# Attention beside a gelu MLP: a constant by memset, weight magnitudes on ScalarE, seven V projections inside the blocks

## The chip, the cores and the metric

The kernel runs on one core of one Trainium2 chip. The metric is the device time of one execution in microseconds; 0.3% of it is 4.5 us. Names used below: TensorE (PE; its weight loads are PEld), VectorE (DVE), ScalarE (ACT), GpSimd (POOL) and SyncE (SP), whose queue issues all of the kernel's DMAs. PSUM has eight banks of 128x512 fp32; TensorE writes there and VectorE and ScalarE read it out.

## The reference

One sequence of 2048 rows and 512 columns. Both branches read the same normalised x.

```python
def _A_ref(x, wqkv, wo):                      # 32 heads of 16
    qkv = (x @ wqkv).reshape(B, S, 3, H, Dh).transpose(2, 0, 3, 1, 4)
    q, k, v = qkv[0], qkv[1], qkv[2]
    scores = jnp.einsum("bhqd,bhkd->bhqk", q, k) * (Dh ** -0.5)
    p = _softmax(scores, axis=-1)
    o = jnp.einsum("bhqk,bhkd->bhqd", p, v)
    return o.transpose(0, 2, 1, 3).reshape(B, S, D) @ wo

def _B_ref(x, w1, b1, w2, b2):                # 512 -> 1792 -> 512
    h = _gelu(jnp.einsum("bsd,df->bsf", x, w1) + b1)
    return jnp.einsum("bsf,fd->bsd", h, w2) + b2

xn = _layernorm(x)
return x + _A_ref(xn, wqkv, wo) + _B_ref(xn, w1, b1, w2, b2)
```

## The kernel before

**Numbers.** Dense products (projections, MLP, output projection) are made in fp16 with every operand split into a high and a low half; `PAIRS` lists the three partial products kept, so a projection of depth 512 is 12 products of 128 rows by 512 columns. Before a weight is split it is scaled by a power of two; `scales` finds it from the largest magnitude. Scores are one fp16 product over stacks: a *stack* (`kst` for keys, `qst` for queries) holds for two heads, in 64 partitions each, the halves of K or Q in 48 rows, and in rows 62 and 63 a constant (`MROW`, 1024, in the keys) against the negative row maximum in two halves (in the queries). Exponentials and V stay in fp32.

**Units.** Work is cut into 512 units: 8 groups of four heads, 4 query blocks of 512, 16 key tiles of 128. A unit u makes four score halves for row maxima (`s_half`, `reduce_max` at L260 on VectorE, tile `mt`), and, 19 units later (`LEAD`), the four transposed score tiles with their exponentials (`e_half`, L305 on ScalarE) and the product with V (`v_half`). The maxima of a block of 16 units are joined at its end (`s_end`, tile `mneg`), turned on TensorE and sent by two DMAs through DRAM into the query stacks.

**Halves.** V products use one half of the array's rows at a time (64 partitions). On the other half, `dense` places products of a dense group, four column tiles each; how many a half unit takes is the group's *pace*: `FAST` is 4, `SLOW` 3, `MEAN` 3 and 4 in turn. So a unit carries 32, 24 or 28 dense column tiles. Groups come from a filler, in this order: Q and K projections for m = 1 to 3 (`rest`), then per query block 14 groups of the first MLP layer and 4 of the second (`mlp`), then the output projection (`tail`). In the units 16 to 18, before the first exponential, `LFILL` places 36 products of the filler's first groups at full width. What the filler has left when the units end is made after them.

**Prologue.** Ahead of the blocks stand the layernorm (`stats`), the transposes of x into `xt` (L799, evacuated at L800 to L806), the projections of Q and K for m = 0 (`project`), all 16 V tiles (`v_proj`, L531, evacuated at L534) and the first 16 units' score halves (`tile_and_unit`). Its order on each engine is found by a planner from estimated costs; from `manual_schedule` on, the order is the one in which the program is written. SP's queue is in order too, and a DMA that waits for a buffer holds those behind it.

**Weights.** The 16 chunks of w1, w2 and wo (512 KB each, tile `wch`, three buffers) are loaded twice: once to find the largest magnitudes (`measure`, two VectorE passes over 128x512 a chunk, L729, tile `amx`), and once to be split on GpSimd (`prepare`, `split_steps`). `MEASURE` says how many passes stand behind each tile of the prologue; the eight passes that are left stand in the first units of the blocks.

**Constants.** `clear` sets both kinds of stacks to zero on GpSimd (L86) and then writes rows 62 and 63 of the key stacks from a small tile by 32 DMAs (L88), 16 for each of two sets of stacks.

Of the kernel before, what the change touches and what calls it, by code (L numbers as in the profile page):

```python
# [1 line left out]

# [15 lines left out]
P = 128  # L18
S = 2048
D = 512  # L20
H = 32
# [8 lines left out]
VW = DH + 1  # L30
LEAD = 19
FAST, MEAN, SLOW = (4, 4), (3, 4), (3, 3)
MEASURE = (3, 0, 1, 2)
HALF = 1300
POOL_NS = 2500
TAIL = 5
LFILL = (8, 16, 12)
WARM = (14, 3, 2, 2)
FINE = "fine"
ORDERED = {mybir.EngineType.SP, mybir.EngineType.PE, mybir.EngineType.Activation, mybir.EngineType.DVE, mybir.EngineType.Pool}  # L40
GELU_C = 0.7978845608028654
GELU_A = 0.044715
MROW = 1024.0
W = 2 * P


@with_exitstack
def layer_kernel(ctx: ExitStack, tc: tile.TileContext, x, wqkv, wo, w1, b1, w2, b2, out):
# [23 lines left out]

    ident = const.tile([P, P], F32, name="ident")
    make_identity(nc, ident)
    ones_row = const.tile([2, P], F16, name="ones_row")
    nc.vector.memset(ones_row, MROW)


    kst, qst = ([[[const.tile([P, QB], F16, name=f"{x}st{i}_{p}_{b}") for b in range(NQB)] for p in range(2)]
# [2 lines left out]
    def clear(i):  # L82
        for b in range(NQB):
            for p in range(2):
                for st in (kst[i][p][b], qst[i][p][b]):
                    nc.gpsimd.memset(st.bitcast(F32), 0.0)  # L86
                for a in range(2):
                    nc.sync.dma_start(kst[i][p][b][64 * a + 62:64 * a + 64, :].rearrange("r (b n) -> r b n", n=P),  # L88
                                      ones_row.unsqueeze(1).to_broadcast([2, 4, P]))

    vv = const.tile([P, NT, H * VW + 15], F32, name="vv")
    nc.gpsimd.memset(vv[:, :, 0:H * VW].rearrange("p t (h e) -> p t h e", e=VW)[:, :, :, DH], 1.0)
# [430 lines left out]
            yield 1.0  # L523
        group.end()

    def v_proj(t, wh, bank):
        pj = bank()
        n = 0
        for c in range(NC):
            for i, j in PAIRS:  # L530
                nc.tensor.matmul(pj, xt[:, i, c, t * P:(t + 1) * P], wh[j][:, c, :], start=(n == 0), stop=(n == 11))  # L531
                n += 1
                yield 1.0
        nc.scalar.activation(vv[:, t, 0:H * VW].rearrange("p (h e) -> p h e", e=VW)[:, :, 0:DH],  # L534
                             pj.rearrange("p (h d) -> p h d", d=DH), AF.Copy)

    def run(gen):
        for _ in gen:
            pass

    pos, spent, cur = [0], [False], [None]
    feed, xbs, wcs = [], {}, {}

    def fetch_x(b):
# [163 lines left out]
    with ExitStack() as st1:  # L708
# [28 lines left out]
        every = [w1v[:, :, i * W:(i + 1) * W] for i in range(7)]  # L737
        every = every + [w2v[:, 2 * i:2 * i + 2, :] for i in range(7)] + [wov[:, 0:2, :], wov[:, 2:4, :]]
        every = every + every
        amx = work.tile([P, 16, 2], F32, name="amx")  # L740
        fac1 = []

        def fetch(k):
# [81 lines left out]
        def some(gen, n):  # L825
            for _ in range(n):
                next(gen, None)

        def measure():

            for n in range(16):
                v = fetch(n)
                for k in range(2):
                    absmax(amx[:, n, k:k + 1], v[:, 2 * k:2 * k + 2, :] if n < 7 else v[:, k, :])
                    yield

        ms = measure()

        def tile_and_unit(t):

            v = v_proj(t, wvh, vbank)
            for k in range(2):
                s_half(t, 2 * k)
                s_half(t, 2 * k + 1)
                some(v, 6)
            s_end(t)
            run(v)

        def weave(*gens):
            gens = list(gens)  # L850
# [76 lines left out]
        run(pq)  # L927
        nc.sync.dma_start(b1_s, b1.rearrange("(f p) -> p f", p=P))
        pos[0] = 16

# [3 lines left out]
        def rest():  # L934
            for k in range(8):
                later(8 + 4 * k, lambda k=k: stacks(1, 1 - k // 4, [k % 4]), True)
            for k in range(4 * NQB):
                c, cols = k % 4, slice(k // 4 * QB, k // 4 * QB + QB)
                later(10 + 3 * k, lambda c=c, cols=cols: nc.sync.dma_start(xn_d[:, :, c, cols], xt[:, :, c, cols]), True)
            for m in range(1, 4):  # L940
                while m not in ready_w:
                    yield None
                if m < 3:
                    by_slots(prep_qk(m + 1, wfs[m + 1], sbank, ready_w))
                for sb in range(NQB):
# [15 lines left out]

        def prepare():
            yield from ms
            am = work.tile([P, 10], F32, name="am_all")
            nc.vector.tensor_reduce(am[:, 0:7], amx[:, 0:7, :], axis=AX.X, op=ALU.max)
            nc.vector.tensor_reduce(am[:, 7:8], b1_s, axis=AX.X, op=ALU.max, apply_absolute_value=True)
            nc.vector.tensor_reduce(am[:, 8:9], amx[:, 7:14, :], axis=AX.XY, op=ALU.max)
            nc.vector.tensor_reduce(am[:, 9:10], amx[:, 14:16, :], axis=AX.XY, op=ALU.max)
            box = []
            yield  # L970
            yield from scales(am, 10, sbank, box)
# [1 line left out]
            fac1.append(fac)  # L973

            nc.vector.reduce_max(gs[:, 0:1], fac[:, 0:8], axis=AX.X)
            nc.vector.tensor_tensor(gs[:, 3:4], fac_v[0][:, 0:1], fac[:, 9:10], op=ALU.mult)
            yield
            nc.vector.reciprocal(gs[:, 1:2], gs[:, 0:1])
            nc.vector.tensor_tensor(gs[:, 2:3], gs[:, 0:1], fac[:, 8:9], op=ALU.mult)
            yield  # L980
            nc.vector.tensor_scalar_mul(gs[:, 1:2], gs[:, 1:2], 0.5)
            ended = [True]
            for n in range(16):
                v = fetch(16 + n)
                while not ended[0]:
                    yield
                ended[0] = False

                def then(wh=None, n=n):
                    ended[0] = True  # L990
                    later(2, lambda: put(wh, n), True)
# [32 lines left out]
    def mlp():  # L1024
# [25 lines left out]
        for b in range(NQB):  # L1050
# [20 lines left out]
            for q in range(4):  # L1071
# [14 lines left out]
                def store(yp, xa=xa, t=t):  # L1086
# [6 lines left out]

                yield Group([lambda f=f, i=i, j=j, q=q, g=g: (g[:, i, f, q * P:(q + 1) * P], w2_s[:, j, f, :])
                             for f in range(NF) for i, j in PAIRS], dbank, store,
                            lambda n, b=b: (b, n // 3) in done, pace=SLOW if b < 2 else MEAN)

    def when(t, fn, n=1):

# [148 lines left out]
```

## Time and profile before

| | |
|---|---|
| median of 3 runs | 1513.81 us (1510.95 to 1516.05) |
| profiled execution | 1513.79 us |
| its span, first to last instruction | 1512.0 us |
| mean granted TensorE clock | 0.993 |
| first exponential starts | 121.85 us |
| last exponential ends | 1495.9 us |
| score maxima (L260) | 2048, 684 ns each, 1304.7 us busy |
| exponentials (L305) | 2048, 598 ns each, 1112.3 us busy |
| GpSimd | 663.7 us busy, 44% |

How to read the lines that follow. In rows of the chain of waits, the first number is the start in us, the second how long this piece set the end, then engine, tile and line, and xN for several merged. Rows of windows begin with a stretch of the span and its length, then for each engine its busy time and, in brackets, its instructions; the last three columns are the granted TensorE clock, the DMA engines' mean busy share and GB/s. Rows of groups give line, engine, operation, tiles and shapes, the count, then busy us and the mean ns of one. Rows of the timeline give start, duration and, in square brackets, how long the engine had been idle and what ended that. SPq is SP's queue: its rows are the issuing of DMAs, not the transfers. A busy TensorE is modelled and overlaps itself; it does not say that TensorE does useful work all the time.

### The profile page before, as it was taken

The page shows a single profiled execution, that of the slowest core. Times are in us where ns is not written, and L with a number is a line of the kernel's source. Part 1 is how long each engine was busy: PE and PEld are TensorE (multiplying, and loading weights), DVE is VectorE, ACT ScalarE, POOL GpSimd, SP SyncE. Part 2 cuts the span into 40 slices and gives each one's busy share as a digit, 9 for nine tenths or more (in the row PEclk, how much of TensorE's full clock was granted, in tenths as well). Part 3 has the DMA queues.
Part 4 walks back from the last instruction along what each step waited for, and adds up shares of the span by engine and source line. Part 5 has one row for each costly group of instructions (what it writes and reads, how often), then busy time and mean ns, then how long its engine had stood idle before and what let it go on. Part 6 is the DMA issues. An engine that isn't in the chain of part 4 may idle for free.

```text
span 1512.0 us, 86779 instructions
## 1 busy us (share of the span) xinstructions
PE 1489.9 (99%) x39407; PEld 822.7 (54%) x39407; DVE 1405.0 (93%) x2368; ACT 1244.0 (82%) x2317; POOL 663.7 (44%) x685
## 2 busy tenths in 40 slices
PE   8999999999999999999999999999999999999998
PEld 4434555555555555555555555555555555555553
DVE  7899999999999999999999999999999999999933
ACT  4326788889998888999888899998889998888885
POOL 4113598637772111777411158761216785211110
PEclk9999999999999999999999999999999999999998
DMA  6454477632222201131011211122102201112422
GB/s 199 132 160 148 148 218 228 195 106 81 67 78 57 70 27 35 44 84 50 22 50 42 65 41 43 36 78 64 34 18 62 79 27 29 49 54 60 131 65 97
DMA packets 113673, 123.75 MB, mean 82 GB/s; under 512 B 24988, under 2 KB 85276, under 8 KB 113304
## 3 DMA queue, kind: packets, MB, share of 16 engines
q1 hardware_dynamic: 113304, 118.21, 25.9%
q8 instruction: 308, 5.05, 1.4%
q14 instruction: 61, 0.50, 0.1%
HBM read 80.61 MB, written 37.34 MB: 78 GB/s over the span
## 4 chain that ended last, share of the span: by engine, by line
PE 81%; DVE 16%; issue 1%; DMA 1%; ACT 1%; POOL 0%; SPq 0%; ACTq 0%; POOLq 0%
PE pV L169 24%; PE pD L169 20%; PE pT L169 17%; PE pS L169 17%; DVE mt L260 14%; PE pT L438 1%; PE pD L438 1%; DVE amx L729 1%; PE pT L531 1%; PE pV L531 0%; DMA wq<-in_A_wqkv_dram 0%; DMA wch<-in_B_w_dram 0%; PE pT L799 0%; PE pS L438 0%; POOL xt L804 0%
## 5 line engine op out<-in xcount | busy, mean ns | idle before, releaser
L260 DVE TENSOR_REDUCE mt<-pS 128x1 f32<-128x512 f32 x2048 | 1304.7, 684 | 41.8 <-PE pS L169 25.9
L305 ACT ACTIVATE pe<-pT 128x512 f32<-128x512 f32 x2048 | 1112.3, 598 | 172.4 <-PE pS L169 82.0
L169 PE MATMUL pV<-pe,vv 64*32 64x512 f32 x8192 | 1076.5, 595 | 0.1
L169 PE MATMUL pT<-qst,kst 64*32 64x512 f16 x8192 | 719.5, 378 | 1.4 <-ACT pe L305 1.2
L169 PE MATMUL pS<-kst,qst 62*32 62x512 f16 x8192 | 624.8, 379 | 6.4 <-DVE mt L260 4.9
L169 PEld LDWEIGHTS <-kst 64*32 64x32 f16 x8192 | 289.4, 91 | 191.8 <-issue 94.2
L169 PEld LDWEIGHTS <-qst 62*32 62x32 f16 x8192 | 274.3, 92 | 206.0 <-issue 60.6
L169 PE MATMUL pD<-w_s,g 64*32 64x512 f16 x5376 | 364.6, 376 | 0.0
L169 PE MATMUL pD<-xb,wc 64*32 64x512 f16 x5376 | 361.1, 377 | 0.0
L169 PEld LDWEIGHTS pV<-pe,vv 64*32 64x32 f32 x8192 | 181.5, 105 | 88.4 <-PE pV L169 4.7
L1090 POOL TENSOR_TENSOR xa<-xa,yt 128x512 f32<-128x512 f32 x16 | 20.5, 1279 | 302.9 <-ACT yt L1088 302.9
L169 PEld LDWEIGHTS <-wc 64*32 64x32 f16 x5376 | 117.0, 91 | 42.7 <-issue 0.5
L169 PEld LDWEIGHTS <-g 64*32 64x32 f16 x5376 | 112.3, 91 | 45.6
L169 PE MATMUL pD<-xt,wqk_h 64*32 64x512 f16 x2016 | 135.9, 380 | 0.6 <-issue 0.4
L361 POOL TENSOR_TENSOR osb<-osb,rb 128x512 f32<-128x512 f32 x31 | 39.9, 1286 | 158.9 <-DMA rb<-den_d 120.3
L1045 POOL TENSOR_TENSOR t<-hh 128x512 f32<-128x512 f32 x56 | 58.3, 1041 | 86.5 <-ACT hh L1065 85.4
L1047 POOL TENSOR_TENSOR t<-t,hh 128x512 f32<-128x512 f32 x56 | 71.9, 1285 | 4.7
L1040 POOL TENSOR_TENSOR t<-t,hh 128x512 f32<-128x512 f32 x56 | 71.9, 1283 | 4.7
L1042 POOL TENSOR_TENSOR g<-t,g 128x512 f16<-128x512 f32 x56 | 65.2, 1165 | 4.7
L1039 POOL TENSOR_SCALAR t<-t,gs 128x512 f32<-128x512 f32 x56 | 39.0, 696 | 49.7 <-ACT t L1034 49.3
L169 PEld LDWEIGHTS <-wqk_h 64*32 64x32 f16 x2016 | 48.5, 92 | 21.5 <-issue 5.4
L169 PE MATMUL pD<-wo_s,oc 64*32 64x512 f16 x828 | 54.5, 378 | 0.0
(141 smaller groups left out, 868.9 us busy)
## 6 DMA issues: line engine op xcount, KB each, us to landing
wch<-in_B_w_dram SPq DMA_DIRECT2D x28, 512.0 KB
wc<-w_d SPq DMA_DIRECT2D x56, 256.0 KB
qk_d<-stg SPq DMA_DIRECT2D x32, 256.0 KB
rb<-den_d SPq DMA_DIRECT2D x124, 64.0 KB
w_d<-wsp SPq DMA_DIRECT2D x28, 256.0 KB
kst<-qk_d SPq DMA_DIRECT2D x128, 48.0 KB
qst<-qk_d SPq DMA_DIRECT2D x128, 48.0 KB
xs<-in_A_x_dram SPq DMA_DIRECT2D x16, 256.0 KB
```

Source lines behind the costliest of these rows:

```text
L169: p = nc.tensor.matmul(*args, **kw)
L260: nc.vector.reduce_max(mt_of[t][:, n, qt, kb:kb + 1], s, axis=AX.X)
L305: nc.scalar.activation(pe, st, AF.Exp, scale=scale_of[g // 2])
L361: pooled((1280, lambda: nc.gpsimd.tensor_tensor(osb, osb, rb, op=ALU.mult)), (620, lambda: nc.gpsimd.tensor_scalar(ot[:, 0], osb, 1.0, 0.0 ...
L438: nc.tensor.matmul(self.bank, lhs, rhs, start=start, stop=self.last and self.over())
L531: nc.tensor.matmul(pj, xt[:, i, c, t * P:(t + 1) * P], wh[j][:, c, :], start=(n == 0), stop=(n == 11))
L1039: pooled((690, lambda: nc.gpsimd.tensor_scalar(t1, t1, 1.0, gs[:, 1:2], op0=ALU.add, op1=ALU.mult)), (1280, lambda: nc.gpsimd.tensor_tenso ...
L1040: (1280, lambda: nc.gpsimd.tensor_tensor(t1, t1, hh, op=ALU.mult)),
L1042: (1160, lambda: nc.gpsimd.tensor_tensor(g[:, 1, f, :], t1, g[:, 0, f, :], op=ALU.subtract)),
L1045: pooled((1040, lambda: nc.gpsimd.tensor_tensor(t1, hh, hh, op=ALU.mult)), (620, lambda: nc.gpsimd.tensor_scalar(t1, t1, 1.0, 1.0 / GELU_A ...
L1047: (1280, lambda: nc.gpsimd.tensor_tensor(t1, t1, hh, op=ALU.mult)),
L1090: add = lambda: nc.gpsimd.tensor_tensor(xa, xa, yt, op=ALU.add)
```

## The change

1. The constant. `clear` fills the key stacks with a pattern of two halves of 1024 by the memset that stood there, and leaves out the tile and the 32 DMAs. Rows 48 to 61 of the key stacks then hold 1024 too; the query stacks are zero there.
2. Magnitudes. For the 16 chunks, the largest magnitude is replaced by the sum of the magnitudes of a partition over 32, made by one ScalarE instruction over the chunk's 1024 columns, with an accumulated output. `MEASURE` becomes (2, 0, 1, 1) chunks a tile, so all 16 stand in the prologue.
3. V projections. Nine of the 16 tiles stay in the prologue, three products after each pair of score halves where six stood. The other seven are groups of 12 products at the head of the filler: the 36 full-width products of units 16 to 18 are now theirs (three tiles), and four tiles go beside V products and score products as halves. `prepare` waits for all V tiles before it splits weights, since the split V weights share their buffers.
4. Paces. The second MLP layer runs at `MEAN` in all query blocks; it ran at `SLOW` in the first two.
5. Two tiny products for `gs` move from VectorE to GpSimd.

```diff
-MEASURE = (3, 0, 1, 2)
+MEASURE = (2, 0, 1, 1)
+NV = 9
+MROWS = struct.unpack("f", struct.pack("ee", MROW, MROW))[0]
+SPREAD = 32.0
-    ones_row = const.tile([2, P], F16, name="ones_row")
-    nc.vector.memset(ones_row, MROW)
...
-                for st in (kst[i][p][b], qst[i][p][b]):
-                    nc.gpsimd.memset(st.bitcast(F32), 0.0)
-                for a in range(2):
-                    nc.sync.dma_start(kst[i][p][b][64 * a + 62:64 * a + 64, :].rearrange("r (b n) -> r b n", n=P),
-                                      ones_row.unsqueeze(1).to_broadcast([2, 4, P]))
+                nc.gpsimd.memset(kst[i][p][b].bitcast(F32), MROWS)
+                nc.gpsimd.memset(qst[i][p][b].bitcast(F32), 0.0)
...
+    def v_group(t, wh, bank):
+
+        def finish(pj):
+            nc.scalar.activation(vv[:, t, 0:H * VW].rearrange("p (h e) -> p h e", e=VW)[:, :, 0:DH],
+                                 pj.rearrange("p (h d) -> p h d", d=DH), AF.Copy)
+            given("act", 600)
+            v_done.append(t)
+
+        return Group([lambda c=c, i=i, j=j: (xt[:, i, c, t * P:(t + 1) * P], wh[j][:, c, :])
+                      for c in range(NC) for i, j in PAIRS], bank, finish)
...
             for n in range(16):
                 v = fetch(n)
-                for k in range(2):
-                    absmax(amx[:, n, k:k + 1], v[:, 2 * k:2 * k + 2, :] if n < 7 else v[:, k, :])
-                    yield
+                dst = am_all[:, n:n + 1] if n < 7 else amx[:, n:n + 1]
+                nc.scalar.activation(v, v, AF.Abs, scale=1.0 / SPREAD, accum_out=dst)
+                yield
...
+        def v_tiles():
+            for t in range(NV):
+                yield from whole(v_group(t, wvh, lambda: (vbank(), None)))
+
+        vs = v_tiles()
+
         def tile_and_unit(t):
 
-            v = v_proj(t, wvh, vbank)
             for k in range(2):
                 s_half(t, 2 * k)
                 s_half(t, 2 * k + 1)
-                some(v, 6)
+                some(vs, NV * 12 // 32)
             s_end(t)
-            run(v)
...
+            for t in range(NV, NT):
+                yield v_group(t, wvh, dbank)
             for m in range(1, 4):
...
-            nc.vector.tensor_tensor(gs[:, 3:4], fac_v[0][:, 0:1], fac[:, 9:10], op=ALU.mult)
+            nc.gpsimd.tensor_tensor(gs[:, 3:4], fac_v[0][:, 0:1], fac[:, 9:10], op=ALU.mult)
...
-            nc.vector.tensor_tensor(gs[:, 2:3], gs[:, 0:1], fac[:, 8:9], op=ALU.mult)
+            nc.gpsimd.tensor_tensor(gs[:, 2:3], gs[:, 0:1], fac[:, 8:9], op=ALU.mult)
...
-                while not ended[0]:
+                while not ended[0] or len(v_done) < NT:
...
-                            lambda n, b=b: (b, n // 3) in done, pace=SLOW if b < 2 else MEAN)
+                            lambda n, b=b: (b, n // 3) in done, pace=MEAN)
```

More of the change, by code (lines that the diff above doesn't have):

```diff
@@ L1 @@
+import struct
 from contextlib import ExitStack
@@ L524, in whole @@
         group.end()
[L526 to L535, printed above, removed]
+    def v_group(t, wh, bank):
[6 more added lines that the diff above has]
+                      for c in range(NC) for i, j in PAIRS], bank, finish)
     def run(gen):
@@ L541, in layer_kernel @@
     pos, spent, cur = [0], [False], [None]
+    v_done = []
     feed, xbs, wcs = [], {}, {}
@@ L739, in layer_kernel @@
         every = every + every
-        amx = work.tile([P, 16, 2], F32, name="amx")
+        amx = work.tile([P, 16], F32, name="amx")
+        am_all = work.tile([P, 10], F32, name="am_all")
         fac1 = []
@@ L927, in layer_kernel @@
         run(pq)
+        run(vs)
         nc.sync.dma_start(b1_s, b1.rearrange("(f p) -> p f", p=P))
@@ L963, in prepare @@
             yield from ms
-            am = work.tile([P, 10], F32, name="am_all")
-            nc.vector.tensor_reduce(am[:, 0:7], amx[:, 0:7, :], axis=AX.X, op=ALU.max)
+            am = am_all
             nc.vector.tensor_reduce(am[:, 7:8], b1_s, axis=AX.X, op=ALU.max, apply_absolute_value=True)
-            nc.vector.tensor_reduce(am[:, 8:9], amx[:, 7:14, :], axis=AX.XY, op=ALU.max)
-            nc.vector.tensor_reduce(am[:, 9:10], amx[:, 14:16, :], axis=AX.XY, op=ALU.max)
+            nc.vector.tensor_reduce(am[:, 8:9], amx[:, 7:14], axis=AX.X, op=ALU.max)
+            nc.vector.tensor_reduce(am[:, 9:10], amx[:, 14:16], axis=AX.X, op=ALU.max)
             box = []
```

## The prediction

> **What bounds the kernel now.** I read the page first: the engine table, then the chain of work that ended last.
>
> ```profile
> PE 1489.9 (99%) x39407; PEld 822.7 (54%) x39407; DVE 1405.0 (93%) x2368; ACT 1244.0 (82%) x2317; POOL 663.7 (44%) x685
> PE 81%; DVE 16%; issue 1%; DMA 1%; ACT 1%; POOL 0%; SPq 0%; ACTq 0%; POOLq 0%
> ```
>
> TensorE sets most of the time and VectorE a sixth. What the change is worth depends on where VectorE does, so I split the run at its first exponential, where the hand-ordered blocks begin. Ahead of it I read the chain of waits in two stretches, and beside it the busy times by stage, up to the row maximum that closes the first block's scores (mneg).
>
> ```profile
> 31.99 2.59 PE pV L531 x12
> ...
> 82.41 1.20 DVE mt L260 x2
> 83.60 0.59 DVE amx L729
> ...
> 85.39 4.44 DMA wch<-in_B_w_dram
> ...
> 108.81 0.13 DVE mneg L271
> ...
> 113.72 0.34 PE pS L169 x8
> ...
> 119.30 0.59 DVE am_qk L462
> ...
> 120.56 1.28 ACT L305
> 121.85 0.61 ACT pe L305
> ```
>
> ```profile
> 29.00:78.00 49.00, 48.68 (x326) 20.20 (x324) 41.86 (x83) 20.66 (x39) 6.95 (x6) 1.00 0.49 145
> 78.00:108.80 30.80, 30.11 (x239) 11.08 (x231) 29.56 (x55) 7.07 (x12) 4.84 (x5) 1.00 0.64 187
> ```
>
> (Columns after the length: PE, PEld, DVE, ACT, POOL, clock, DMA share, GB/s.) To 78 us the chain is TensorE's: V products follow each other at 2.59/12 = 0.216 us. From 78 to 109 it is VectorE's: score maxima (0.60 each) with weight maxima (0.59) between them. ScalarE is busy 27.7 of 79.8 us.
>
> **The change, part by part.** *Prologue.* 84 of 192 V products leave it, and the weight maxima leave VectorE.
>
> ```profile
> 38.00:78.00 40.00, 5.03 (x8) 1.00 0.46 130
> 78.00:110.00 32.00, 10.71 (x16) 1.00 0.62 180
> 122.00:142.00 20.00, 3.35 (x5) 0.91 0.45 135
> ```
>
> (Busy time of L729 alone.) In the built order three V products now follow each pair of score halves, where six did. In the first stage, with 16 pairs, TensorE loses 48 x 0.216 = 10.4 us: 49.0 - 10.4 = 38.6. VectorE needs 41.9 - 5.0 = 36.8. In the second stage TensorE has 60 V products and 16 pairs at 0.34, 13.0 + 5.4 = 18.4, and VectorE 29.6 - 10.7 = 18.9. The floor is 38.6 + 18.9 = 57.5, 22.3 under today's 79.8. In-order queues never fill both engines: VectorE is busy (41.9 + 29.6)/79.8 = 89% today. Its remaining 55.7 us at 89% make 62.5, so I take -17. Behind mneg stand 36 full-width products (now V, before Q and K) and six score pairs, unchanged at about 9.8 us, then one evacuation, the table load and the exponential; the two magnitudes that end that stretch (119.30 and a weight maximum behind it, 0.6 each) are gone from there: -1.
>
> ScalarE takes over 16 absolute sums over 128x1024. The nearest row of that shape is a scaled copy; the two VectorE passes it replaces were 674 ns each.
>
> ```profile
> L145 ACT ACTIVATE wvh<-wch,inv 128x1024 f16<-128x1024 f32 x2 | 2.2, 1187 | 0.0
> L729 DVE TENSOR_REDUCE amx<-wch 128x1 f32<-128x512 f32 x32 | 21.1, 674 | 0.9 <-DMA wch<-in_B_w_dram 0.9
> ```
>
> 16 x 1.19 = 19 us on an engine with 52 idle hides in those stages if the chunks are there; uncovered it would cost those 19. The Trainium skill, ScalarE: Activation LUTs, "Rules for kernel authors", speaks against the move: simple arithmetic belongs on VectorE, which it puts at up to about three times faster (in 16 bits). The trace does not agree for this fp32 shape: 1.19 us against 2 x 0.674 on VectorE. What the rule would make of the time is a rival below.
>
> Waiting is the danger. In the new order the first sum stands on ScalarE between the two scalings of the second x block, ahead of the evacuations that feed the next transposes.
>
> ```profile
> 8.17 12.63 SPq L88 DMA_DIRECT2D kst<-ones_row  x16
> 15.51 0.42 PE L799 MATMUL pT<-ident,xs 128*128 128x128 f32 x1
> 22.88 1.33 ACT L784 ACTIVATE xs<-xs,sd 128x512 f32<-128x512 f32 x2
> 28.31 2.49 SPq L404 DMA_DIRECT2D kst<-qk_d  x4
> 61.93 0.44 SPq L723 DMA_DIRECT2D wch<-in_B_w_dram  x1
> ```
>
> With the constant's first 16 DMAs gone from SP's queue, the next x loads need not wait for their end at 20.8; the transposes of the first x block release the buffers at about 15.5, and the first weight chunk goes out six DMAs later (four of x, two of weights, at the 2.49/4 = 0.62 of 28.31), at about 19.2, where today the first goes out at 61.93. A chunk lands in about 4.4 us (the wait at 85.39), so the sum ends near 25 and the second scaling starts some 2 us after today's 22.88: +2. Queued behind it are that scaling, five xt and pf evacuations and the split of V's weights; TensorE's transposes and the Q and K products wait for those. SP queues behind the second chunk too: it needs the first sum done, and the first key stacks are issued after it, near 28.3 as today. The other 16 have only the third x block's projections behind them, which are not computed yet when they end: nothing. A memset of 1024.0 costs what one of zero does (same instruction and size), on GpSimd, idle there: nothing.
>
> First exponential: 121.85 - 17 - 1 + 2 = 105.9, a change of -16. Bounds: TensorE's 10.4 alone with 2 us of waits, -8; both engines full and no wait, -24.
>
> *First units of the blocks.* Five weight maxima remain there now (3.35 us), and two tiny products take long:
>
> ```profile
> 152.52 0.99 DVE L976 TENSOR_TENSOR gs<-fac,fac 128x1 f32<-128x1 f32 x1
> 155.89 2.07 DVE L979 TENSOR_TENSOR gs<-gs,fac 128x1 f32<-128x1 f32 x1
> 158.62 0.40 PE L169 MATMUL pS<-kst,qst 62*32 62x512 f16 x4 [1.63 <-DVE mt L260]
> ```
>
> ```profile
> 121.85:362.20 240.35, 182.79 (x337) 0.99 0.53 164
> ```
>
> (Units 19 to 102 as they are; busy time of the exponentials.) The two go to GpSimd, where nothing of that stretch waits for them. VectorE loses up to 6.1 us of a stretch it binds; TensorE waits 1.63 us for it behind the second one. I take -5 of it for units 19 to 102; bounds -9 (a further 3 us, about one scale chain's stall, now ahead of the blocks) and 0. The new wait for all V tiles holds the weight splits to about unit 31, some 70 units before the first layer reads them: nothing. Behind the V groups the Q and K groups end 21 units later (unit 102, not 81), but their stacks are needed only at unit 128.
>
> *Rates.* The built order gives each unit its dense products; the total of units is fixed. With 4 exponentials a unit, less one that straddles the edge:
>
> ```profile
> 440.00:588.00 148.00, 123.69 (x228) 1.00 0.18 49
> 589.00:715.00 126.00, 102.15 (x189) 1.00 0.20 58
> 994.00:1118.00 124.00, 102.15 (x189) 1.00 0.18 49
> 1413.00:1489.00 76.00, 60.85 (x113) 1.00 0.29 91
> ```
>
> Second layer at SLOW: 148/56.75 = 2.608 us a unit. First layer: 126/47 = 2.681. Second layer at MEAN: 124/47 = 2.638. Tail: 76/28 = 2.714. Of the 428 units from 104 on, before are 175 first layer, 112 SLOW, 96 MEAN, 45 tail: 469.2 + 292.1 + 253.2 + 122.1 = 1136.6. After: 196, 0, 192, 40: 525.5 + 506.5 + 108.6 = 1140.6, so +4. The 84 moved products thus cost 0.05 us apiece, not 0.216, their cover being the V half on the other rows. Bounds 0 (MEAN no dearer) and +9 (MEAN at the first layer's rate).
>
> *End.* Five units of output projection are pushed past the old end; the order shows them beside the last V halves, except 20 column tiles (five groups of four) behind the last transposes, where TensorE waits anyway.
>
> ```profile
> 1491.28 2.18 ACT L305 ACTIVATE pe<-pT 128x512 f32<-128x512 f32 x4 [0.25 <-PE pT L169]
> 1493.71 2.18 ACT L305 ACTIVATE pe<-pT 128x512 f32<-128x512 f32 x4 [0.25 <-PE pT L169]
> 1502.80 5.30 PE L438 MATMUL pD<-wo_l,ot 64*128 64x512 f16 x12 [0.68 <-ACT ot L391]
> ```
>
> The last four units now take 2.43 with little dense work and would take 2.71: +1.1. Five groups at 0.216 against 0.68 idle: +0.4 to 1.1. I take +1.7; bounds 0.5 and 4.8 (all 88 additional tiles bare, 22 x 0.216).
>
> Sum: -16 - 5 + 4 + 1.7 = -15.3. The profiled execution took 1513.79 (span 1512.0 and 1.8 around it), the median is 1513.81, so 1513.8 - 15.3 = **1498.5 us**.
>
> **The rivals.** *ScalarE's order eats half of it.* If the sums' waits delay transposes and evacuations a few times more, the exponential comes at 114: 1513.8 - 8 - 5 + 5.7 = 1506.5. For it: one wait of 4.44 us for a chunk in today's chain, and 16 chunks now asked for in the time of 13. Against: they start at 19.2 us, not at 61.93. The Trainium skill, TensorE: Matmul & The Clock Gate (its specification table), calls ScalarE's queue a strict FIFO; by that nothing overtakes a waiting sum, and this rival keeps its chance, though no run yet shows ScalarE waiting for a chunk.
>
> *The chunks become the bound (slower).* The first exponential stands behind the 16th sum on ScalarE, the chunks share three buffers, and SP's queue stops at each that is not free. One chunk at a time costs 4.44 + 1.19 = 5.6 us: 19.2 + 16 x 5.6 = 109, still earlier than today. It decides above 6.5 us a chunk; at 7, the exponential comes at 131 plus 3 for the second group's scales and the table: 1513.8 + 12.3 + 0.7 = 1526.8. For it: DMA share 0.64 in the second stage already. Against: 187 GB/s there would bring 512 KB in 2.8 us.
>
> *ScalarE is slow at it (slower).* At three times VectorE's 1.35 us a chunk, 16 x 4.05 + 27.7 = 92.5 us would stand in place of 62.5: 1528.5. For it no row, against it the 1.19.
>
> *Both engines fill.* Exponential at 98, and -9 in the blocks: 1513.8 - 24 - 9 + 5.7 = 1486.5. For it: two engines with equal loads and three score banks between them. Against: 89% today.
>
> That the halves are not hidden, as the change says, costs 84 x 0.216 = 18.1 instead of 4: 1512.6, no change; the row of 2.681 for full dense units speaks against it.
>
> **How the numbers follow.** Forecast (1491 to 1503) 0.52; half eaten 0.20; both full 0.13; not hidden 0.07; chunks bind 0.07; ScalarE slow 0.01. The time is the first one's, 1498.5. The range 1487 to 1509 takes in the rivals at 1506.5 and nearly all of 1486.5, and leaves the other three out. A difference under 0.3% (4.5 us) can't be told from none; faster by more has 0.52 + 0.20 + 0.13 = 0.85, the same 0.07, slower 0.08.
>
> **What would show it.** First exponential at 98 to 114; the stretch before it with VectorE and TensorE both over 85% busy and no pure VectorE chain of maxima; no ScalarE wait over 5 us for a chunk. Units 19 to 102 in about 235 us (240.35 today); second layer of the first two blocks at 2.63 a unit. The work behind the last exponential of the units 1 to 2 us longer. I am wrong if the chain ahead of the first exponential passes through weight chunks or ScalarE's sums, or if units with V halves take over 2.8 us.

## The result and the profile after

The changed kernel takes 1510.68 us (median of 22 runs, 1507.67 to 1517.12), the kernel before 1515.6 us (median of 22, 1510.95 to 1522.63). The ratio is 0.9971, 95% interval 0.9963 to 0.998: 4.4 us faster, where 15.3 were predicted. The interval leaves out 1, so there is a gain, but it is no larger than the 0.3% that the prediction counted as none. The profiled execution took 1509.1 us (span 1507.3 and 1.8 around it).

The engine table and the chain of waits on the page of the changed kernel:

```profile
PE 1484.6 (98%) x39995; PEld 815.2 (54%) x39995; DVE 1387.1 (92%) x2333; ACT 1257.4 (83%) x2348; POOL 661.4 (44%) x686
PE 87%; DVE 8%; issue 1%; DMA 1%; ACT 1%; POOL 0%; SPq 0%; ACTq 0%; POOLq 0%
```

VectorE's share of the chain falls from 16% to 8%, and TensorE's rises from 81% to 87%: the chain changes hands, as forecast, and the kernel gets little shorter.

Split at the same places as in the prediction (windows of the exponentials, first the kernel before, then the changed one; the busy time is ScalarE's in them):

```profile
121.85:362.20 240.35, 182.79 (x337) 0.99 0.53 164
364.83:1380.43 1015.60, 834.17 (x1536) 1.00 0.17 50
1380.43:1495.89 115.46, 93.22 (x173) 1.00 0.29 89
```

```profile
108.54:347.01 238.47, 182.74 (x337) 1.00 0.45 139
349.46:1373.76 1024.30, 833.47 (x1537) 1.00 0.20 54
1373.76:1490.32 116.56, 93.36 (x172) 1.00 0.28 86
```

The rows are units 19 to 102, 104 to 487, and 488 to the last exponential. So the first exponential comes 13.3 us earlier (121.85 to 108.54), units 19 to 102 win 1.9, units 104 to 487 lose 8.7, the rest of the units loses 1.1, and 0.9 more lies behind the last exponential (17.0 for 16.1). Together with unit 103 that is the 4.7 us between the spans. The gain ahead of the blocks is there; of the 15.2 us won up to unit 102, 9.8 are given back in the units behind it.

Ahead of the blocks, the stages of the changed kernel (columns as in the prediction: PE, PEld, DVE, ACT, POOL, clock, DMA share, GB/s):

```profile
29.00:78.00 49.00, 47.85 (x342) 18.30 (x341) 40.49 (x80) 34.71 (x64) 8.10 (x7) 1.00 0.77 232
78.00:94.30 16.30, 16.30 (x120) 4.97 (x121) 13.98 (x28) 4.28 (x7) 3.67 (x4) 1.00 0.28 85
94.30:108.54 14.24, 14.23 (x141) 5.49 (x140) 10.12 (x22) 3.68 (x6) 0.00 (x0) 1.00 0.41 125
```

The row maximum that closes the first block (mneg) stands at 94.30, where it stood at 108.81. To there TensorE is busy 64.2 of 65.3 us and VectorE 54.5, or 83%. From 78 us to the first exponential the chain of waits is TensorE's (28.6 of 30.5 us). Ahead of that it passes twice through the load of a weight chunk for the sums on ScalarE, 8.7 us in all:

```profile
16.71 4.80 DMA wch<-in_B_w_dram
...
47.84 1.03 ACT wch L835 x2
48.89 3.95 DMA wch<-in_B_w_dram
```

### The profile page after: what moved, and what is told of

Read it like the earlier page. It is cut to its first block, busy times and chain, and to the rows that moved or that the text cites. A ratio compares the mean times of both kernels' runs of the same rounds, so it can differ in the third digit from the quotient of the medians.

```text
span 1507.3 us, 87890 instructions
## 1 busy us (share of the span) xinstructions
PE 1484.6 (98%) x39995; PEld 815.2 (54%) x39995; DVE 1387.1 (92%) x2333; ACT 1257.4 (83%) x2348; POOL 661.4 (44%) x686
## 3 DMA queue, kind: packets, MB, share of 16 engines
q8 instruction: 312, 5.11, 1.4%
## 4 chain that ended last, share of the span: by engine, by line
PE 87%; DVE 8%; issue 1%; DMA 1%; ACT 1%; POOL 0%; SPq 0%; ACTq 0%; POOLq 0%
PE pV L168 25%; PE pD L168 23%; PE pS L168 18%; PE pT L168 18%; DVE mt L259 7%; PE pT L437 1%; PE pD L437 1%; DMA wch<-in_B_w_dram 1%; PE pV L437 1%; DMA wq<-in_A_wqkv_dram 0%; DVE am_qk L461 0%; DVE mneg L270 0%; PE pT L800 0%; ACT xt L801 0%; DVE wvh L145 0%
## 5 line engine op out<-in xcount | busy, mean ns | idle before, releaser
L168 PEld LDWEIGHTS <-qst 62*32 62x32 f16 x8192 | 280.8, 92 | 230.4 <-issue 62.8
L168 PEld LDWEIGHTS <-kst 64*32 64x32 f16 x8192 | 279.3, 91 | 174.9 <-issue 79.1
L168 PE MATMUL pD<-w_s,g 64*32 64x512 f16 x5376 | 359.4, 377 | 0.0
L168 PE MATMUL pD<-xt,wqk_h 64*32 64x512 f16 x2304 | 152.5, 378 | 1.5 <-issue 1.5
L168 PEld LDWEIGHTS <-wqk_h 64*32 64x32 f16 x2304 | 53.4, 92 | 23.2 <-issue 4.6
L168 PE MATMUL pD<-wo_s,oc 64*32 64x512 f16 x828 | 54.5, 378 | 0.0
```

The lines of the kernel that those rows point to most:

```text
L168: p = nc.tensor.matmul(*args, **kw)
```

## Experiments

Stage times from the profiles, in us. "Ahead" is the first exponential, "late" goes from unit 104 to the last exponential, "behind" is the rest of the span; unit 103 (2.4 to 3.6) lies between.

| kernel | ahead | units 19-102 | late | behind | span | ratio to before (95%) |
|---|---|---|---|---|---|---|
| before | 121.85 | 240.35 | 1131.1 | 16.1 | 1512.0 | 1 |
| before_again | 122.28 | 244.30 | 1130.7 | 16.9 | 1516.8 | one run |
| changed | 108.54 | 238.47 | 1140.9 | 17.0 | 1507.3 | 0.9971 (0.9963-0.998) |
| e1_stacks_early | 110.80 | 235.37 | 1137.2 | 18.2 | 1504.0 | 0.9945 (0.9925-0.9965) |
| e2_max_dve | 123.67 | 238.07 | 1139.1 | 17.6 | 1521.6 | 1.0057 (1.0041-1.0073) |
| e2b_max_dve_placed | 119.46 | 242.33 | 1139.8 | 17.9 | 1522.0 | 1.006 (1.0039-1.0081) |
| e3_v_prologue | 128.05 | 239.40 | 1132.7 | 16.2 | 1518.9 | 1.0021 (1.0009-1.0033) |
| e4_slow | 112.39 | 238.09 | 1134.1 | 29.1 | 1516.2 | 1.002 (1.0005-1.0035) |
| e5_paced | 110.13 | 240.77 | 1138.0 | 15.2 | 1507.8 | 0.9987 (0.9972-1.0001) |
| e6_ones_dma | 120.56 | 239.17 | 1139.5 | 15.2 | 1516.9 | 1.0047 (1.003-1.0065) |
| e11_tied2 | 107.51 | 237.19 | 1138.4 | 16.8 | 1502.3 | 0.9948 (0.9928-0.9967) |
| e12_memset_alone | 118.87 | 243.33 | 1131.2 | 17.1 | 1513.1 | 0.999 (0.9976-1.0005) |
| e13_traffic | 108.71 | 252.64 | 1137.9 | 15.2 | 1517.0 | 1.0007 (0.9991-1.0023) |
| e14_tied2_nv8 | 107.35 | 237.01 | 1139.2 | 18.5 | 1505.1 | 0.9921 (0.9904-0.9938) |

Five of them (changed, e1, e4, e5, e13) run the same program ahead of the first exponential and have it at 108.5 to 112.4, 110.1 on the mean. One profile fixes that stage to about 2 us, no better; "behind" moves by 3 us between kernels with the same end (e1 and e5).

**The stack loads of the third group of heads (e1).** In the changed kernel unit 114 takes 4.85 us where others take 2.6. TensorE's rows there, then SyncE's in the 9 us up to it:

```profile
377.86 0.40 PE L168 MATMUL pS<-kst,qst 62*32 62x512 f16 x4
380.22 0.43 PE L168 MATMUL pT<-qst,kst 64*32 64x512 f16 x8 [1.96 <-DMA qst<-m_d]
```

```profile
370.97 4.60 SPq L403 DMA_DIRECT2D qst<-qk_d  x8
375.67 1.66 SPq L284 DMA_DIRECT2D m_d<-mhl  x2
378.61 1.15 SPq L289 DMA_DIRECT2D qst<-m_d  x4
```

The scores of the next block need its negated maxima, which go through memory (m_d). Their row maximum is taken at 370.13 in unit 111, but SyncE issues eight stack loads first, and the first write of the maxima follows after 5.54 us, where it mostly follows after 1.8 to 2.0 (2.42 is the longest of the later blocks). Those loads are not needed before unit 128. They go out one set a unit from unit 86 in the kernel before, in the loop that holds the MLP; that loop now begins at unit 104, because the Q and K projections end 21 units later, and its first eight units run right into unit 111.

In e1 the function that issues them is also called in the loop ahead of that one (its definition moves up as it is):

```diff
...
         while not spent[0] or more or cur[0] is not None:
+            more_stacks()
             unit(fil)
...
```

> The changed kernel, but the eight stack loads of the third group of heads may go out from unit 86 on, as they did before the change, and not only from unit 104 on. Theory (SyncE's queue): those loads stood ahead of the DMAs of the negated maxima, so unit 114 had to wait for its queries' maxima (1.96 us idle on TensorE). The maxima's first DMA then follows the row maximum of unit 111 after 1.8 to 2.0 us in place of 5.54, unit 114 takes 2.6 in place of 4.85, and the kernel is 2.2 us shorter. Rival (the DMA itself was slow there, whatever stood ahead of it): unit 114 keeps at least 1 us of its excess and the time does not move.

The same view of e1_stacks_early, whose row maximum of unit 111 is taken at 369.29:

```profile
371.25 1.22 SPq L284 DMA_DIRECT2D m_d<-mhl  x2
373.67 1.16 SPq L289 DMA_DIRECT2D qst<-m_d  x4
```

The write follows after 1.96 us and unit 114 takes 2.55. Four other kernels of the table have the late loads too, at slightly other times: in e2, e4, e6 and e2b the write follows after 2.70, 3.47, 4.40 and 5.44 us, and unit 114 takes 2.56, 3.82, 4.10 and 4.61. Shown: the 2.3 us were SyncE's queue, and they are lost only where the loads meet the write. The ratio goes from 0.9971 to 0.9945; the intervals overlap a little, the trace does not leave room for doubt about unit 114.

**The sums, back on VectorE (e2, e2b).**

```diff
...
-                dst = am_all[:, n:n + 1] if n < 7 else amx[:, n:n + 1]
-                nc.scalar.activation(v, v, AF.Abs, scale=1.0 / SPREAD, accum_out=dst)
+                for k in range(2):
+                    absmax(amx[:, n, k:k + 1], v[:, 2 * k:2 * k + 2, :] if n < 7 else v[:, k, :])
...
```

> The changed kernel with the weights' magnitudes as absolute maxima on VectorE again (two passes of 0.67 us for each chunk, 32 in all), the V halves left in the blocks. Theory A (VectorE bound the prologue, the sums bring most of its gain): the first exponential comes at 117 to 121 in place of 108.5. Theory B (with the V products gone TensorE is the bound and VectorE has room): at 109 to 113. In both the units after it are as in the changed kernel, within 2 us.

The first exponential came at 123.67, above theory A's range and later than before the change. Four units of the prologue (88 to 110 us) held 16 of the 32 weight maxima, and the chain passes through them:

```profile
97.59 1.78 DVE mt L259 x3
99.37 2.37 DVE amx L729 x4
...
112.68 3.28 PE pT L437 x8
```

The last row is the price of the wait: eight products in 3.28 us, 0.41 each where 0.216 is usual. TensorE had idled:

```profile
90.00:108.00 18.00, 9.54 (x68) 2.51 (x68) 17.18 (x34) 1.93 (x3) 3.66 (x4) 0.64 0.63 202
```

It is busy 9.5 of 18 us, and the granted clock is 0.64 on the mean: 1.00 up to 95 us and 0.50 from there to 115. The Trainium skill, TensorE: Matmul & The Clock Gate, "Part 1: The HAM clock gate", has the clock halved after an idle window of about 3.4 us. The halving agrees; such an idle window is not in the trace, where the longest idle time of TensorE in this stretch is 3.34 us and ends at 103.38, when the clock is already down. Since the placing was itself in doubt, e2b placed the halves as before the change:

> As e2_max_dve, but with each half of a chunk's maximum placed as before the change (3, 0, 1 and 2 halves after each unit, so that eight of the 32 are left for the blocks), since in e2_max_dve all 32 stood ahead of the blocks. Theory A (VectorE binds as long as the maxima are on it, wherever they stand): first exponential at 115 to 120, and some 2 to 4 us more in units 19 to 66. Theory B (only the placing made e2_max_dve slow): at 108 to 112.

119.46, with 2.3 us more in units 19 to 65: theory A. As long as the maxima are on VectorE, taking V products out is worth nothing ahead of the blocks as far as one profile of each can tell, since the memset alone has the first exponential at 118.87 (e12, below), and it costs its share later.

**V back ahead of the blocks (e3).** The edit is `NV = 16`.

> The changed kernel with all 16 V projections ahead of the blocks again, the sums on ScalarE kept. Theory A (VectorE bound the prologue): the first exponential at 110 to 114. Theory B (TensorE did: 84 products of 0.216 us come back, 18 us at most): at 117 to 124. In both the units from 104 on get shorter by 4 to 7 us against the changed kernel, since 21 units' worth of halves leaves them, and unit 114 takes 2.6 us, since the projections of the queries and keys end about 12 units sooner and the stack loads with them.

128.05: above both ranges, 6 us later than before the change, although VectorE has lost its maxima. Theory A falls; B was right in kind, not in size. It is 19.5 us later than in the one profile of the changed kernel and 18.0 later than the mean of the five, which is no more than the 84 products themselves (18.1). But the kernel before carried these products and the maxima, and was there at 122. So ScalarE is in it too (its waits in all, how many, the longest):

```profile
ACT wch L835 <- DMA wch<-in_B_w_dram: 12.3, 9, 4.9
```

The sums wait for their chunks, 12.3 us where the changed kernel waits 7.5, and evacuations and scalings stand behind them; the chain passes through two of the loads, 11.6 us. No run parts the share of TensorE from that of ScalarE. Units 104 on get 8.2 us shorter than in the changed kernel, a little over the expected 4 to 7, 2.3 of them unit 114.

**The slower pace again (e4).** The edit is `pace=SLOW if b < 2 else MEAN`.

> The changed kernel with the second layer of the first two blocks at 3 and 3 products again. Theory (the faster pace is what keeps the moved halves off the end): some 16 units of output projection, 64 products of 0.216 us, are pushed behind the last exponential, +13.8 there, while 80 units of second layer lose 0.07 us on every second one, -3; net +8 to +11. Rival (the end has room for them): within 2 us of the changed kernel.

The units from 104 on win 6.8 us, 2.5 of them in the tail and 1.0 at unit 114 (3.82), and 12.1 more lie behind the last exponential:

```profile
1496.18 10.48 PE pD L437 x48
```

Those 48 are output projections that no longer fit beside the units. By medians it is 7.2 us slower than the changed kernel (1517.84): the theory, just under its range.

**The constant by DMA again (e6).**

```diff
...
-                nc.gpsimd.memset(kst[i][p][b].bitcast(F32), MROWS)
...
+                for a in range(2):
+                    nc.sync.dma_start(kst[i][p][b][64 * a + 62:64 * a + 64, :].rearrange("r (b n) -> r b n", n=P),
+                                      ones_row.unsqueeze(1).to_broadcast([2, 4, P]))
```

> The changed kernel with the constant rows of the key stacks written by 32 DMAs again in place of the memset's value. Theory (the sixteen DMAs of the first half hold SyncE's queue from about 8 to 21 us, and the x loads and first weight chunk behind them): first exponential 2 to 6 us later. Rival (nothing waits for them that long): within 1.5 us of 108.5 to 112.4, which is where three profiles of the same prologue have it.

120.56: ten microseconds over the mean of the like prologues, nearly the whole gain, where the theory had 2 to 6. SyncE's queue in e6_ones_dma, then in the changed kernel:

```profile
7.17 13.07 SPq L92 DMA_DIRECT2D kst<-ones_row  x16
42.25 10.66 SPq L92 DMA_DIRECT2D kst<-ones_row  x16
59.68 0.45 SPq L728 DMA_DIRECT2D wch<-in_B_w_dram  x1
```

```profile
12.32 1.77 SPq L717 DMA_DIRECT2D xs<-in_A_x_dram  x4
16.71 0.50 SPq L723 DMA_DIRECT2D wch<-in_B_w_dram  x1
```

With the DMAs in it, the first weight chunk goes out at 59.68 and not at 16.71; the sixteen sums then run from 69.0 to 108.5, one every 2.6 us. SyncE issues the load of a bias (b_s) behind the last chunk, VectorE reduces it as soon as it lands, and the last score maxima ahead of the first exponential stand behind that. The chain (its "issue" is an idle time of GpSimd for which the profile shows no wait):

```profile
73.48 19.09 issue
...
96.89 4.96 DMA wch<-in_B_w_dram
...
105.05 5.07 DMA b_s<-in_B_b_dram
```

So the memset is what lets the sums run early. Is it worth the same alone? e12 is the kernel before with it:

> The kernel before with the memset alone: no DMA writes the constant rows, all else as before. Theory (in the old order the maxima on VectorE bind, and nobody is waiting for the loads behind those DMAs): first exponential at 119 to 122, the time within 0.2% of before. Rival (the queue that is free from 8 to 21 and from 43 to 54 us is worth the same here as in the changed kernel, about 10 us): first exponential at 110 to 114.

118.87, just under the theory's range and far above the rival's: 3 us, and no difference in the time (0.999). The parts of the change do not add up, each needs the others: with all three the first exponential comes at 110, with any one taken back at 119.5 to 128. With the memset in place, four kernels set the other two parts apart: with neither it comes at 118.87 (e12), with the V products moved alone at 119.46 (e2b), with the sums alone at 128.05 (e3), with both at 110.1 (mean of five). Alone, one gains nothing and the other loses 9 us; together they gain 9.

**Waits on ScalarE (e11, e14).** In the changed kernel a sum costs 1.057 and 0.189 us (activation, and reading the accumulator) and waits of 7.5 us in all stand before six of them:

```profile
L835 ACT ACTIVATE wch<-wch x16: 1047/1057/1102, 21.5 to 82.3; 128x1024 f32<-128x1024 f32 x16
L835 ACT ACTIVATION_READ_ACCUMULATOR wch<-wch x16: 185/189/243, 22.5 to 83.3; 128x1 f32 x16
...
  DMA wch<-in_B_w_dram: 4.4, 4
  DMA wch<-in_A_wo_dram: 3.1, 2
```

e11 keeps them behind the scalings:

```diff
...
-                nc.scalar.activation(v, v, AF.Abs, scale=1.0 / SPREAD, accum_out=dst)
+                if not n:
+                    nc.vector.tensor_scalar(even, xs[11][:, 0:1], 0.0, 1.0 / SPREAD, op0=ALU.mult, op1=ALU.add)
+                nc.scalar.activation(v, v, AF.Abs, scale=even, accum_out=dst)
...
```

> The kernel with the early stack loads, and the factor of the sums taken from a small tile that is made (as zero times the data plus 1/32) from the last scaled row tile of the third x block, so that no sum can stand on ScalarE ahead of the scalings of the second to third blocks. Theory (waits for chunks on ScalarE's in-order queue delay the scalings and what follows): the first exponential comes at 104 to 108 in place of 108.5 to 112.4, and no wait of ScalarE for a chunk stands in the chain. Rival (with the sums pushed together at the end the chunks' loads bind): 112 to 120. Third case (TensorE bound it anyway): no change, 108.5 to 112.4.

107.51, inside the theory's range but only 1 us under the earliest of the five like prologues and 2.6 under their mean. The chain ahead of it holds no load of a weight chunk any more, as the theory said; in the other four like prologues such loads hold 4.0 to 10.9 us of it, in the changed kernel 8.7. The whole kernel does not show the gain: its median is 1505.2 us, that of e1, which it starts from, 1506.92 (0.9948 and 0.9945). One more V projection out (`NV = 8`):

> e11_tied2 with one more V projection moved into the blocks (8 left ahead of them). Theory (TensorE still bounds the stretch ahead of the first exponential): 12 products of 0.216 us leave it, first exponential 2 to 2.6 us earlier (about 105), and 1 to 1.5 us come back in the blocks and at the end: net -1. Rival (no engine alone bounds it any more): first exponential within 1 us of 107.5, net +1.

107.35: the first exponential does not move, the rival is right there. Its time is nevertheless the best seen, 1503.45 us (0.9921, 0.9904 to 0.9938); its interval overlaps e11's, and its profile, taken in the slowest of its six runs (1506.93), does not say why it should be better, so of the two only this is shown: both beat the kernel before and the changed one's median.

**Idle time that no wait explains (before_again, e5, e13).** Units 31 to 65 took 100.5 us before and 105.7 in the changed kernel. TensorE's waits between unit 31 and unit 82, kernel before first:

```profile
PE pS L169 <- DVE mt L260: 1.6, 1, 1.6
PE pD L169 <- issue: 0.4, 1, 0.4
```

```profile
PE pD L168 <- issue: 1.5, 3, 0.6
PE pS L168 <- issue: 1.3, 2, 0.9
PE pT L168 <- issue: 0.7, 1, 0.7
```

"issue" is idle time for which the profile shows no wait. The page has a DMA queue that carries instructions (q8, 312 packets of 16 KB, one for each 256 of TensorE's matmuls and weight loads, one every 4.4 us in these units). Worked from the starts of its packets and a count of TensorE's instructions, the six idle times of the changed kernel:

```
idle at  us    unit  fetch started   count  since the fetch before
169.60   0.91  40    1.5 us earlier  385    5.8 us
188.64   0.34  47    2.2             358    5.5
207.10   0.62  53    1.8             391    7.4
212.48   0.35  55    1.9             359    5.2
222.04   0.71  58    1.7             399    5.8
241.76   0.54  64    1.8             383    6.6
```

The count is the number of instructions that TensorE had started beyond 256 for each fetch before; the higher it is, the later the fetch. Over units 31 to 81 of all fourteen profiles its median is 279. Of the 448 fetches there 65 started at 357 or later (a limit chosen with the counts in view), and 51 of the 65 were followed within 2.3 us by an idle time of over 0.3 us; of the other 383 fetches 3 were, and those were waits for VectorE's maxima. All 51 idle times stand at the same place, where the same count has come to 449 or 450, and end 2.2 to 2.6 us behind the start of the late fetch. So TensorE had used up its instructions there and went on when the next packet had come. Data packets took 75% or more of the DMA engines' time in the 4 us ahead of each fetch in the table, as around 205 us:

```profile
q1 hardware_dynamic: 1010, 1.32, 96.4%
q8 instruction: 1, 0.02, 1.5%
```

Over the 448 fetches, where data packets took under 60% of the DMA engines' time in the 4 us ahead, 1 fetch of 191 came late; where they took more, 64 of 257. So late fetches come where data fill the DMA engines, which does not yet make the data their cause. Whether it belongs to the change, a second profile of the kernel before had to say:

> The kernel before once more, for a second profile of its stages. If the first profile stands for it: first exponential within 1 us of 121.85, units 31 to 65 in 100 to 101.5 us with at most one idle time of TensorE over 0.3 us that no wait explains. If it was a lucky one: first exponential or these units 2 us or more longer, with two or more late fetches.

```profile
PE pD L169 <- issue: 2.1, 2, 1.3
PE pT L169 <- issue: 1.6, 1, 1.6
PE pS L169 <- issue: 0.4, 1, 0.4
```

Four of five late fetches (366 to 429) stopped TensorE, for 4.1 us in all, and units 31 to 65 took 105.3 us; in e12, which has the old order there, they took 104.7. The profile of before on which the prediction was built was a lucky one, and the change is not to blame. Pacing the weights and copies was to take the cause away:

```diff
...
-                later(10 + 3 * k, lambda c=c, cols=cols: nc.sync.dma_start(xn_d[:, :, c, cols], xt[:, :, c, cols]), True)
+                later(10 + 5 * k, lambda c=c, cols=cols: nc.sync.dma_start(xn_d[:, :, c, cols], xt[:, :, c, cols]), True)
...
+                while pos[0] < 31 + 4 * n:
+                    yield
...
```

> The kernel with the early stack loads (e1_stacks_early), and the copies out of normalized x and the splitting of the weights spread over units 29 to 104 (a copy every 5 units in place of 3, a weight chunk every 4 units in place of about 2.2). Theory (TensorE's instructions are fetched by the same DMA engines, and a fetch comes too late where data fills them): the idle times of TensorE of over 0.3 us that no wait explains between units 31 and 82 (6 with 3.5 us in the changed kernel, 3 with 1.8 us in e1_stacks_early) go to none or one, and units 31 to 65 take 97 to 100 us in place of 102 to 106; units 66 to 102 stay within 1 us of 101. Rival (the idle times come from the order of work, or only move with the traffic): units 31 to 102 together take the same 203 to 207 us.

The idle times that no wait explains went down to one (0.63 us, behind a late fetch), as the theory said, but so few stand in the first profile of before as well, and the time failed: units 31 to 102 took 209.3 us. Two more idle times to unit 81 are waits for VectorE's maxima, and the traffic that was moved reached the next block's maxima (SyncE, and 3.31 us idle in unit 98):

```profile
325.92 4.58 SPq L403 DMA_DIRECT2D qst<-qk_d  x8
330.54 2.79 SPq L356 DMA_DIRECT2D rb<-den_d  x4
...
334.41 2.03 SPq L284 DMA_DIRECT2D m_d<-mhl  x2
```

The maximum of unit 95 was taken at 327.78 and written 6.6 us later: unit 114's stall at another place. The reverse test added traffic, `later(50 + k // 2, ...)` with 32 copies to a spare place:

> The kernel with the early stack loads, and 32 more copies of normalized x (256 KB each, to a place that nobody reads), two for each unit from about 68 to 84, where e1_stacks_early has no unexplained idle time of TensorE after 260 us and a DMA share of 0.28. Theory (a fetch of TensorE's instructions comes late where data fill the DMA engines): at least two idle times of over 0.3 us appear in units 68 to 86, each 1 to 2.2 us behind the start of a fetch that comes 360 or more instructions behind its usual place (200 to 350), and these units get 2 to 5 us longer. Rival (the lateness belongs to the order of the work in units 31 to 66): none appears, at most 1 us.

The stretch got 12 us longer, more than either theory said, and only one of its three idle times (0.89 us, unit 72) follows a late fetch (381). The others are waits for data:

```profile
277.14 0.40 PE L169 MATMUL pS<-kst,qst 62*32 62x512 f16 x4 [2.45 <-DVE mt L260]
303.78 0.64 PE L169 MATMUL pT<-qst,kst 64*32 64x512 f16 x8 [5.96 <-DMA qst<-m_d]
```

By the measure set beforehand (two late fetches) the theory is not borne out. What stands is the count above: late fetches stop TensorE. That data traffic makes them late fits the rows (64 of 257 against 1 of 191), but neither taking it away nor adding it has shown it, and it stays open.

## Why the prediction was wrong

*What bounds it.* Right in kind: VectorE's chains of maxima are gone, and from 78 us on TensorE sets the pace up to the blocks. Ahead of that the chain changes engines and waits twice for a weight chunk.

*Prologue, -16.* Measured -13.3 in the profile, and -12 between means (122.1 before, two profiles; 110.1 after, five). Inside the bounds of -8 to -24, but 3 to 4 us short, and this is one of the two steps that failed. Up to mneg the forecast was 91.5 and 2 of waits, against 94.3: the premise of VectorE busy at 89% failed; it had 83%. Behind mneg it was 14.2 us and not 12.1; nine V products, the last of them ending 1.3 us behind the start of that row maximum, stood on TensorE ahead of the transposes of it, and the first write of the maxima followed after 3.35 us where it took 1.81 before:

```profile
93.52 2.05 PE pV L437 x9
```

The +2 was for one wait. The second scaling does stand 2.3 us behind the end of the first, for the wait and the sum, but it starts at 22.59, no later than the 22.88 of before, so against before it cost less than the 2. The chain shows a second one, at 48.89, that the sum left out; only the rival of ScalarE's order had more than one. Against the mean of the like prologues e11 puts what ScalarE's waits cost at about 2.6 us, with one profile and a spread of 2 us. The absolute sum itself was priced about right (1.19), 1.25 us on ScalarE against two passes of 0.674, so the Trainium skill's rule (ScalarE: Activation LUTs, "Rules for kernel authors"), which is given for 16 bits, does not carry over to this shape. The Trainium skill's strict order of ScalarE's queue (TensorE: Matmul & The Clock Gate) agrees with the trace: the second scaling waited behind the first sum. "A memset costs nothing" was right and beside the point: what mattered was that 32 DMAs leave SyncE, 10 us in e6, where the second 16 of them, put at nothing, stand ahead of the first weight chunk. The prediction used it for the early chunks, but priced only the harm of these.

*First units, -5.* Measured -1.9 in the profile, but -5.0 between the means of like kernels (242.3 before, two; 237.3 for changed, e1 and e4). The gain stands where the maxima and the two tiny products had been: units 19 to 30 take 31.5 us in these three, against 38.4 and 37.0 in the two profiles of before and 38.5 in e12. With five of the weight maxima back there, as before (e2b), they take 33.3; the two products were never taken back alone, so their share is not shown. The term was right; its base was a profile with one stop for instructions where another has four.

*Rates, +4, and end, +1.7.* This is the other step that failed, and the larger. Measured +9.8 in the units and +0.9 behind them. Set against the same kinds of units before, the mix of units 104 to 487 after costs about 1020 us at the old prices, some 4.5 more: the composition was right. e3 against before gives part of it alone (V ahead of the blocks, second layer at 3 and 4): +1.6 to the last exponential, and e1 against e3 the moved halves: +4.5, or 0.054 us for each of the 84 products, as estimated (0.05). The rest is unit 114, 2.3 us, and some 1.4 scattered between e1 and the changed kernel. The sentence that failed was the one on the Q and K groups, "their stacks are needed only at unit 128", taken to be worth nothing: when they are needed was right, what they stand in front of was not asked. Without that stall (e1, 1506.92 us) the time lies inside the range.

*The rivals.* "ScalarE's order eats half" has the first exponential at 114 and the time at 1506.5; the mean of 110 lies midway between it and the forecast's 105.9, and e11 puts the waits at about 2.6 us of that. Nearest to the median is "halves not hidden" with 1512.6, but by luck, as its mechanism is not there (e3). "The chunks become the bound" is what e6 shows once the memset is gone (120.56, a sum every 2.6 us up to the end); with it, no ScalarE wait for a chunk passes 2.1 us. Of what was to be seen, some came as said: the first exponential between 98 and 114, no chain of maxima, no ScalarE wait over 5 us, the second layer at 2.64 us a unit. VectorE was at 83% and not over 85, and units 19 to 102 took 238.5 us and not 235. And one sign of being wrong came true: the chain ahead of the first exponential passes through weight chunks and ScalarE's sums.

*The total.* The misses against the profile of before are 2.7 ahead of the blocks, 3.1 in units 19 to 102 (its luck), 4.7 to the last exponential and 0.3 behind: 10.8, all of one sign, less 0.2 in unit 103, from 1498.5 to the 1509.1 of the profiled execution. The range took the sum's terms as if their errors would cancel. The starting point was low as well: the median of before is 1513.8 us over the three runs of the forecast and 1515.6 over 22.

## What to carry to other kernels

When work is moved, list what its end releases: here a loop that began 21 units later pushed loads in front of an urgent DMA on an in-order queue, though the loads themselves had time. Price a change of several parts as a whole, and ask of each part whether the others live on it: a memset that did not show in the time by itself was the condition for ten microseconds. Take a second profile of the starting point before a forecast of 1%: one stage of it moved by 5 us between two executions.

## What was not expected of the hardware

TensorE's instructions arrive by DMA during the run, about 16 KB every 4.4 us in these blocks (312 packets, 5.11 MB in all), and one that starts about a hundred instructions late mostly (51 of 65) stops TensorE within 2.3 us, for up to 2.1 us, in nearly all cases (49) without any wait in the profile. All 51 stops came at the same instruction count, 449 or 450 beyond 256 for each fetch before. The granted clock fell to 0.50 in a prologue stage of e2 where TensorE was busy 9.5 of 18 us, and products there took 0.41 us for 0.216, so that a wait is paid a second time.
